# Output projection with five Strassen units in place of four: where the sums are made, which bank takes which product, and the order of the stage

## The chip, the core and the metric

The kernel runs on one core of a Trainium2 chip. The metric is the device time of one execution in microseconds (us). Three runs of the kernel before took 751.25, 751.36 and 752.31 us; the median is 751.36 us.

Five engines work side by side, each through its own instruction stream in order: TensorE (PE in the profile; PEld is its weight load), VectorE (DVE), ScalarE (ACT), GpSimd (POOL) and SyncE (SP, which here issues transfers). An instruction that must wait holds up everything behind it on its engine.

## The reference

```python
def _A_ref(x, wqkv, wo):                 # x: 1 x 2048 x 1024, 32 heads of 32
    q, k, v = split(x @ wqkv)
    phi = lambda t: where(t > 0, t + 1, exp(t)) + 1e-6
    pq, pk = phi(q), phi(k)
    kv = einsum("bhsd,bhse->bhde", pk, v)
    z = einsum("bhsd->bhd", pk)
    num = einsum("bhqd,bhde->bhqe", pq, kv)
    den = einsum("bhqd,bhd->bhq", pq, z)[..., None] + 1e-6
    return merge_heads(num / den) @ wo

def _B_ref(x, w_gate, w_up, w_down):     # 1024 -> 3584 -> 1024
    return (silu(x @ w_gate) * (x @ w_up)) @ w_down

xn = layernorm(x)
s = _A_ref(xn, wqkv, wo)
g = silu(_B_ref(xn, w_gate, w_up, w_down))
out = x + s * g
```

All tensors are bfloat16. The change lies in the last step of `_A_ref`, the product with `wo` (the output projection), which makes `s`.

## The kernel before, in words

The 2048 tokens are four blocks b = 0 to 3 of 512, each of four tiles t of 128 tokens. A 1024-wide row is eight chunks of 128 (G, DC); `wo` is cut into two column halves of 512 (CW), and HG = 4 is half of the chunks.

**Phase 1** makes the normalized, transposed input and the keys and values of all blocks (matmuls at L546) and sums them to KVZ (L568). **Phase 2** then goes through the blocks. `emit_Q` (L178 to 185) makes 128 columns of the queries of one block by eight matmuls into a PSUM tile, and `emit_phi` (L144 to 164) applies phi: for b > 0 three ACT steps (L148, L149, L150), then one DVE step (L151). `emit_ND` (L725 to 751) makes one tile's numerators and denominators with eight matmuls (L735) into the PSUM tile `nd`, then DVE divides: L739 and L743 make the reciprocals, L747 (three instructions) writes the quotient o. `nd` comes from a pool with one buffer of three PSUM banks (L387), so a later `nd` group waits until DVE has read an earlier one. `emit_OT` (L753 to 756) has SP issue a transposing transfer of o into `oT`, the left operand of the output projection.

**The output projection has two forms.** Directly, `emit_S` (L758 to 772): for one tile and one column half eight matmuls of 128x512 (L766), an ACT eviction with a scale (L769), and after the second half a store to `s_dram` from ACT's queue (L772). Blocks 0 and 1 go this way. Or as a unit of Strassen's method in Winograd's form, `s_unit` (L785 to 848): two token tiles together, seven products of four matmuls each (L808, called from `mmk`) where the direct form has 32 matmuls. The tiles of blocks 2 and 3 go this way, as pairs (0, 2) and (1, 3). A unit needs

- four differences of `wo`'s quarters, `To_sb`, made once by GpSimd (L774 to 780);
- four sums of `oT`'s quarters (`sums`, L801 to 804), made by DVE into a part of `wq_sb` that is no longer used (`so`) and, the fourth, in place into `oT`;
- four PSUM banks out of the five `fx`: X and Y change places from unit to unit, Z is always `fx[2]`, W is `fx[3]` or `fx[4]`.

Its products, by their names in the code: **x** into X, after which ACT copies X to Y (L814); **w** into W, after which ACT makes w1 (L821); **y** adds into Y, after which ACT copies Y to Z (L826) and makes s2 (L827); **x2** adds into X, evicted by ACT (L831); **z** adds into Z, evicted by DVE with w1 added (L835); **z2** adds further into Z, evicted by ACT (L840); **w2** adds into W, evicted by DVE with s2 added (L845). A tile's store is issued by SP (`out_s`, L852). The tiles w1 and s2 come from the pool `phiw`, whose tags "r_t" and "e_t" have two buffers each.

**The order is written out by hand.** PE, DVE, ACT and POOL run their instructions in program order (the manual schedule at L384), and SP too in this phase (L693). So the sequence of calls in L893 to L939 is the order of every engine. `run` takes a list of query groups and direct halves and puts the `nd` groups of the block before between them. After the last query group, L899 to L915 write out the tail of the direct form and the first unit, and L916 to L939 run the other three units from strings of steps: a bare name is a step of the unit n, "-" ahead of a name a step of the unit before it, `sums` the sums of the unit after, `nd` the next `nd` group with its transpose, `new` opens a unit, `Ssum` and `p` the DVE sums over the FFN's input (L688 to 692), `silu` loads ACT's table for the FFN.

Beside this, `prep_step` prepares the FFN's weights: DVE scales a tile (L311), GpSimd makes four differences of it (L323 to 326), and a store and further loads are issued. **Phase 3** is the FFN, the larger part of the kernel; its first products come from `emit_a` (L975), by matmuls at L958, with evictions at L985 and L986.

Of the kernel before, what the change touches and what calls it, by code (L numbers as in the profile page):

```python
# [9 lines left out]
ACT = mybir.ActivationFunctionType  # L10
ALU = mybir.AluOpType
FP32 = mybir.dt.float32
BF16 = mybir.dt.bfloat16
I32 = mybir.dt.int32
F32R = mybir.dt.float32r
F16 = mybir.dt.float16
# [5 lines left out]
def kernel(  # L22
# [11 lines left out]
    nc = tc.nc  # L34
    P = 128
    x2 = A_x.flatten_outer_dims()
    out2 = out.flatten_outer_dims()
    S, D = x2.shape
# [4 lines left out]
    DC = D // P  # L43
# [4 lines left out]
    TPB = TB // P  # L48
    CW = min(512, D)
# [48 lines left out]
    marks = {}  # L98
# [25 lines left out]
    wq_sb = w12.tile([P, DC, D], BF16, name="wq_sb")  # L124
# [8 lines left out]
    s_sc = persist.tile([P, 1], FP32, name="s_sc")  # L133
# [35 lines left out]
    phiw = p12.enter_context(tc.tile_pool(name="phiw", bufs=2, reuse_waits="tile"))  # L169
# [221 lines left out]
    with ExitStack() as p1:  # L391
        wpool = p1.enter_context(tc.tile_pool(name="p1w", bufs=1, reuse_waits="tile"))
        work = p1.enter_context(tc.tile_pool(name="p1work", bufs=2, reuse_waits="tile"))
# [222 lines left out]
        HG = G // 2  # L616
# [97 lines left out]
    with ExitStack() as p2:  # L714
# [43 lines left out]
        def emit_S(b, t, cc, bank=None):  # L758
            oT = oT_tiles[b]
            ttok = slice(t * P, (t + 1) * P)  # L760
            if (b, t) not in s_tiles:
                s_tiles[(b, t)] = work.tile([P, D], BF16, name="s_sb", tag="s_sb")
            s_sb = s_tiles[(b, t)]
            s_ps = bank or ps2.tile([P, CW], FP32, name="s_ps", tag="B2")
            for c in range(G):
                mm = nc.tensor.matmul(s_ps[:], lhsT=oT[:, c, ttok], rhs=wo_sb[:, c, cc * CW:(cc + 1) * CW],  # L766
                                      start=(c == 0), stop=(c == G - 1))
                marks.setdefault(("S", b, t), mm)
            nc.scalar.activation(out=s_sb[:, cc * CW:(cc + 1) * CW], in_=s_ps[:], func=ACT.Copy, scale=s_sc[:])  # L769
            if cc == NCC - 1:  # L770
                r0 = b * TB + t * P
                nc.scalar.dma_start(out=s_dram[r0:r0 + P, :], in_=s_tiles.pop((b, t))[:])  # L772
# [9 lines left out]
        fx = []  # L782
        unit_n = [0]

        def s_unit(b, u):  # L785
            n = unit_n[0]
            unit_n[0] += 1
            oT = oT_tiles[b]
            t1, t2 = u, u + 2
            k1, k2_ = slice(t1 * P, (t1 + 1) * P), slice(t2 * P, (t2 + 1) * P)  # L790
            a11, a12 = oT[:, 0:HG, k1], oT[:, HG:G, k1]
            a21, a22 = oT[:, 0:HG, k2_], oT[:, HG:G, k2_]
            b11, b21, b22 = wo_sb[:, 0:HG, 0:CW], wo_sb[:, HG:G, 0:CW], wo_sb[:, HG:G, CW:D]
            X, Y, Z, W = fx[n % 2], fx[1 - n % 2], fx[2], fx[3 + n % 2]
            so = wq_sb[:, TPB:DC, :].rearrange("p a b -> p (a b)")[:, (n % 2) * 2048:(n % 2) * 2048 + 3 * HG * P]
            so = so.bitcast(F16).rearrange("p (q k t) -> p q k t", q=3, k=HG)
            S4 = a21.bitcast(F16)
            sb = {}

            def sums():  # L800
                nc.vector.tensor_tensor(out=so[:, 0], in0=a21, in1=a22, op=ALU.add)  # L801
                nc.vector.tensor_tensor(out=so[:, 1], in0=so[:, 0], in1=a11, op=ALU.subtract)
                nc.vector.tensor_tensor(out=so[:, 2], in0=a11, in1=a21, op=ALU.subtract)
                nc.vector.tensor_tensor(out=S4, in0=a12, in1=so[:, 1], op=ALU.subtract)

            def mmk(out, a_, b_, first):
                for k in range(HG):
                    mm = nc.tensor.matmul(out[:], lhsT=a_[:, k, :], rhs=b_[:, k, :], start=first and k == 0,  # L808
                                          stop=k == HG - 1, skip_group_check=True)
                return mm  # L810

            def x():
                marks[("S", b, u)] = mmk(X, a11, b11, True)
                nc.scalar.copy(out=Y[:], in_=X[:])  # L814

            def w():
                for t in (t1, t2):
                    s_tiles[(b, t)] = work.tile([P, D], BF16, name="s_sb", tag="s_sb")
                mmk(W, so[:, 0], To[0], True)
                sb["w"] = phiw.tile([P, CW], FP32, name="w1", tag="r_t")  # L820
                nc.scalar.activation(out=sb["w"][:], in_=W[:], func=ACT.Copy, scale=s_sc[:])  # L821

            def y():
                mmk(Y, so[:, 1], To[1], False)
                s2 = sb["s2"] = phiw.tile([P, CW], FP32, name="s2", tag="e_t")
                nc.scalar.copy(out=Z[:], in_=Y[:])  # L826
                nc.scalar.activation(out=s2[:], in_=Y[:], func=ACT.Copy, scale=s_sc[:])  # L827

            def x2():
                mmk(X, a12, b21, False)  # L830
                nc.scalar.activation(out=s_tiles[(b, t1)][:, 0:CW], in_=X[:], func=ACT.Copy, scale=s_sc[:])  # L831

            def z():
                mmk(Z, so[:, 2], To[2], False)
                nc.vector.scalar_tensor_tensor(out=s_tiles[(b, t2)][:, CW:D], in0=Z[:], scalar=s_sc[:],  # L835
                                               in1=sb["w"][:], op0=ALU.mult, op1=ALU.add)

            def z2():
                mmk(Z, a22, To[3], False)
                nc.scalar.activation(out=s_tiles[(b, t2)][:, 0:CW], in_=Z[:], func=ACT.Copy, scale=s_sc[:])  # L840
                out_s(b, t2)

            def w2():
                mmk(W, S4, b22, False)
                nc.vector.scalar_tensor_tensor(out=s_tiles[(b, t1)][:, CW:D], in0=W[:], scalar=s_sc[:],  # L845
                                               in1=sb["s2"][:], op0=ALU.mult, op1=ALU.add)
                out_s(b, t1)
            return dict(sums=sums, x=x, w=w, y=y, x2=x2, z=z, z2=z2, w2=w2)

        def out_s(b, t):  # L850
            r0 = b * TB + t * P
# [22 lines left out]
        def mix(a, b_):  # L874
            r = []
            for k in range(max(len(a), len(b_))):
                r += a[k:k + 1] + b_[k:k + 1]
            return r

        def sh(b, hf):  # L880
            return [s_item(b, t, cc) for t in (2 * hf, 2 * hf + 1) for cc in range(NCC)]

        def run(body, at, b, order=(0, 1, 2, 3)):
            for k, f in enumerate(body):
                f()
                if k in at:
                    nd_item(b, order[at.index(k)])()
                phi_flush()

        def qs(b):  # L890
            return [q_item(b, g) for g in range(G)]

        run(qs(1), (1, 3, 5, 7), 0)  # L893
        q = qs(2)
        run(q[:2] + mix(q[2:], sh(0, 0) + sh(0, 1)), (1, 4, 7, 10), 1)
        q = qs(3)
        run(q[:2] + mix(q[2:], sh(1, 0)), (1, 4, 7, 10), 2, (0, 2, 1, 3))
        nds = [nd_item(3, t) for t in (0, 2, 1, 3)]
        emit_S(1, 2, 0)  # L899
        emit_S(1, 2, 1)  # L900
        fx.extend([ps2.tile([P, CW], FP32, name="fx%d" % k, tag="B2") for k in range(5)])
        units = [s_unit(2, 0), s_unit(2, 1)]
        u = units[0]
        nds[0]()
        u["x"]()
        u["sums"]()
        emit_S(1, 3, 0, fx[4])
        nds[1]()
        emit_S(1, 3, 1, fx[2])
        u["w"]()  # L910
        units[1]["sums"]()
        u["y"]()
        u["x2"]()
        nds[2]()
        u["z"]()  # L915
        parts = []  # L916
        for n in range(1, 4):
            u, v = units[n - 1], units[n]
            for st in ('x w nd new -z2 sums y -w2 x2 z', 'x w new Ssum -z2 sums p y -w2 x2 z p', 'x w -z2 y p -w2 z x2 p z2 silu w2')[n - 1].split():
                if st == "nd":  # L920
                    nds[3]()
                elif st == "new":
                    units.append(s_unit(3, n - 1))
                elif st == "sums":
                    units[n + 1]["sums"]()
                elif st == "p":
                    parts.pop(0)()
                elif st == "silu":
                    nc.scalar.preload_act_table(ACT.Silu)
                elif st == "Ssum":  # L930
                    blk_es.close()
                    blk12_es.close()
                    sp = ctx.enter_context(tc.tile_pool(name="p3S", bufs=1, side="right", reuse_waits="tile"))
                    emit_Ssum(passes[0], parts)
                    stat_ps[0] = lambda: psa_tile("st_ps3")[0][:, 0, 511:512]
                    prep_flush()
                elif st[0] == "-":
                    u[st[1:]]()
                else:  # L939
                    v[st]()  # L940
# [990 lines left out]
```

## Time and profile before

| | us |
|---|---|
| median of three runs | 751.36 |
| time of the profiled execution | 751.34 |
| its span in the trace | 749.6 |
| PE busy | 741.9 |
| PEld busy | 370.8 |
| DVE busy | 590.6 |
| POOL busy | 403.2 |
| ACT busy | 385.6 |
| first matmul of the stage's last query group starts / first FFN matmul starts | 208.88 / 244.28 |

The granted TensorE clock was 1.00 over the whole span. Times inside the trace count from the start of the span, in us; the profiled execution's own time is 1.7 us longer than the span. The rows used below have, in this order, start, duration, engine, line, operation, output<-inputs with partitions x elements and type, and the number of instructions taken together; a matmul's duration overlaps that of the next one, so the distance of starts tells PE's pace. In brackets stands idle time of the engine ahead of the row, and what ended it. POOL, DVE and ACT lines can be held against PE's by their start times, since all share one clock of the trace.

### The profile page before, as it was taken

The page shows a single profiled execution, that of the slowest core. Times are in us where ns is not written, and L with a number is a line of the kernel's source. Part 1 is how long each engine was busy: PE and PEld are TensorE (multiplying, and loading weights), DVE is VectorE, ACT ScalarE, POOL GpSimd, SP SyncE. Part 2 cuts the span into 40 slices and gives each one's busy share as a digit, 9 for nine tenths or more (in the row PEclk, how much of TensorE's full clock was granted, in tenths as well). Part 3 has the DMA queues.
Part 4 walks back from the last instruction along what each step waited for, and adds up shares of the span by engine and source line. Part 5 has one row for each costly group of instructions (what it writes and reads, how often), then busy time and mean ns, then how long its engine had stood idle before and what let it go on. Part 6 is the DMA issues. An engine that isn't in the chain of part 4 may idle for free.

```text
span 749.6 us, 11280 instructions
## 1 busy us (share of the span) xinstructions
PE 741.9 (99%) x3962; PEld 370.8 (49%) x3962; DVE 590.6 (79%) x1046; ACT 385.6 (51%) x556; POOL 403.2 (54%) x435
## 2 busy tenths in 40 slices
PE   8999999999999999999999999999999999999997
PEld 3544444454454444444444444644444444467665
DVE  6577788887697688788889886587877767688897
ACT  5677866889965666667557511232222232322023
POOL 0111799998640255858586027310766676770076
PEclk9999999999999999999999999999999999999999
DMA  9957799869678668787889417998698889668854
GB/s 316 337 139 149 219 329 307 310 151 263 208 202 273 229 223 289 274 322 279 320 270 417 169 48 295 269 373 282 225 306 305 307 290 347 244 221 315 279 172 92
DMA packets 132425, 194.21 MB, mean 259 GB/s; under 512 B 36384, under 2 KB 106144, under 8 KB 122640
## 3 DMA queue, kind: packets, MB, share of 16 engines
q1 hardware_dynamic: 123600, 158.69, 65.3%
q0 software_dynamic: 7328, 32.31, 11.6%
q10 hardware_dynamic: 1440, 2.49, 1.0%
q8 instruction: 31, 0.51, 0.3%
q14 instruction: 26, 0.21, 0.1%
HBM read 122.68 MB, written 63.96 MB: 249 GB/s over the span
## 4 chain that ended last, share of the span: by engine, by line
PE 94%; DVE 3%; DMA 1%; ACT 1%; issue 1%; POOL 1%; DVEq 0%; ACTq 0%; POOLq 0%; SPq 0%
PE zw L958 25%; PE kv_ps L546 15%; PE xb L958 13%; PE q_ps L183 6%; PE dzw L1252 6%; PE yb L958 6%; PE dm L1533 5%; PE dm L1497 3%; PE fx L808 3%; PE s_ps L766 3%; PE dx L1252 2%; PE dy L1252 2%; PE dm L1252 1%; PE kvz L568 1%; PE nd L735 1%
## 5 line engine op out<-in xcount | busy, mean ns | idle before, releaser
L958 PEld LDWEIGHTS <-w_sb 128*128 128x128 f16 (+1 forms) x1568 | 152.0, 98 | 183.1 <-issue 0.5
L958 PE MATMUL xb<-xnT,w_sb 128*128 128x512 bf16 x448 | 115.0, 379 | 0.0
L546 PE MATMUL kv_ps<-wkv_sb,xnT 128*128 128x512 bf16 x512 | 113.8, 379 | 0.6 <-ACT xnT L535 0.4
L958 PE MATMUL zw<-xnT,w_sb 128*128 128x512 bf16 x448 | 105.9, 379 | 0.0
L958 PE MATMUL zw<-S,w_sb 128*128 128x512 f16 x448 | 105.8, 379 | 0.0
L323 POOL TENSOR_TENSOR w_sb<-w_sb 128x512 f16<-128x512 bf16 x42 | 50.7, 1206 | 99.9 <-DVE w_sb L311 51.2
L288 ACT ACTIVATE w_sb<-w_sb 128x2048 bf16<-128x2048 bf16 x42 | 79.9, 1902 | 3.5 <-DMA w_sb<-in_B_w_up_dram 2.4
L546 PEld LDWEIGHTS <-xnT 128*128 128x128 bf16 x512 | 48.3, 97 | 56.0 <-ACT xnT L535 0.8
L1139 POOL TENSOR_TENSOR w_sb<-w_sb 128x512 f16<-128x512 f16 (+3 forms) x48 | 50.0, 1063 | 28.5 <-DMA w_sb<-wd 27.5
L1034 ACT ACTIVATE sg<-cg 128x1024 bf16<-128x1024 f32 x28 | 29.6, 1057 | 57.6 <-DVE cg L1027 57.6
L183 PE MATMUL q_ps<-xnT,wq_sb 128*128 128x512 bf16 x256 | 58.4, 379 | 0.4 <-DVE pqT L151 0.4
L958 PE MATMUL yb<-S,w_sb 128*128 128x512 f16 x224 | 57.5, 379 | 0.0
L1027 DVE SCALAR_TENSOR_TENSOR cg<-zw,rc_all,s 128x1024 f32<-128x1024 f32 x28 | 35.9, 1283 | 25.3 <-PE zw L958 12.8
L986 DVE SCALAR_TENSOR_TENSOR s<-yb,rc_all,s 128x512 f32<-128x512 f32 x42 | 31.4, 749 | 27.9 <-ACT s L985 27.9
L324 POOL TENSOR_TENSOR w_sb<-w_sb 128x512 f16<-128x512 bf16 x42 | 50.7, 1207 | 3.3
L1230 POOL DMA_DIRECT2D out_dram<-io x16 | 8.7, 544 | 80.7 <-DVE io L1229 80.5
L326 POOL TENSOR_TENSOR w_sb<-w_sb 128x512 f16<-128x512 bf16 x42 | 50.3, 1197 | 0.0
L325 POOL TENSOR_TENSOR w_sb<-w_sb 128x512 f16<-128x512 bf16 x42 | 49.8, 1185 | 0.0
L985 ACT ACTIVATE s<-xb,rcl 128x512 f32<-128x512 f32 x14 | 9.6, 687 | 65.0 <-PE xb L958 65.0
L985 ACT ACTIVATE s<-xb,rc_all 128x512 f32<-128x512 f32 x42 | 28.4, 675 | 21.9 <-issue 12.7
L311 DVE TENSOR_SCALAR w_sb<-w_sb,cs_all 128x2048 bf16<-128x2048 bf16 x35 | 36.2, 1035 | 3.5 <-DVE cs_all L301 0.8
L183 PEld LDWEIGHTS <-wq_sb 128*128 128x128 bf16 x256 | 24.4, 97 | 28.1 <-issue 0.6
(232 smaller groups left out, 1364.4 us busy)
## 6 DMA issues: line engine op xcount, KB each, us to landing
w_sb<-pk_g SPq DMA_DIRECT2D x27, 1024.0 KB, 6.4
pk_g<-w_sb SPq DMA_DIRECT2D x14, 1024.0 KB, 5.0
w_sb<-pk_u SPq DMA_DIRECT2D x14, 1024.0 KB, 8.5
pk_u<-w_sb POOLq DMA_DIRECT2D x13, 1024.0 KB, 5.5
w_sb<-l SPq DMA_DIRECT2D x12, 896.0 KB, 5.6
l<-w_sb POOLq DMA_DIRECT2D x9, 896.0 KB, 7.7
w_sb<-in_B_w_gate_dram SPq DMA_DIRECT2D x14, 512.0 KB, 6.6
w_sb<-in_B_w_down_dram SPq DMA_DIRECT2D x28, 256.0 KB, 4.7
```

The source lines that it names most:

```text
L183: nc.tensor.matmul(q_ps[:], lhsT=wq_sb[:, dc, g * P:(g + 1) * P], rhs=xn_ap(dc, btok), start=(dc == 0), stop=(dc == DC - 1))
L288: nc.scalar.activation(out=junk, in_=raw_view(key, t), func=ACT.Square, accum_out=asum[:])
L323: nc.gpsimd.tensor_tensor(out=T1, in0=b12, in1=b11, op=ALU.subtract)
L324: nc.gpsimd.tensor_tensor(out=T2, in0=b22, in1=T1, op=ALU.subtract)
L325: nc.gpsimd.tensor_tensor(out=T3, in0=b22, in1=b12, op=ALU.subtract)
L326: nc.gpsimd.tensor_tensor(out=T4, in0=b21, in1=T2, op=ALU.subtract)
L546: mm = nc.tensor.matmul(kv_ps[:], lhsT=xn_ap(dc, tok), rhs=wkv_sb[:, dc, c * CW:(c + 1) * CW], start=(dc == 0), stop=(dc == DC - 1))
L958: mm = nc.tensor.matmul(out, lhsT=lhs(k), rhs=rhs(k), start=(first and k == 0), stop=(k == HK - 1), skip_group_check=True)
L985: nc.scalar.activation(out=s1[:], in_=x_[:], func=ACT.Copy, scale=rc)
L1139: nc.gpsimd.tensor_tensor(out=b(o_), in0=b(a_), in1=b(b_), op=ALU.subtract)
L1252: nc.tensor.matmul(out, lhsT=lhs, rhs=rhs, start=first, stop=lastk, skip_group_check=True)
L1533: nc.tensor.matmul(out, lhsT=lhs, rhs=w[:, j], start=i == 1 and j == 0, stop=j == NQ - 1, skip_group_check=True)
```

## The change

- **A fifth unit.** Tiles 2 and 3 of block 1 become a unit, the new first one, in place of four calls of `emit_S` (two tiles, two halves). Units now are 0: block 1, tiles (2, 3); 1 and 2: block 2, tiles (0, 2) and (1, 3); 3 and 4: block 3, tiles (0, 2) and (1, 3).
- **Sums by GpSimd.** `s_unit` takes an engine for its sums. Units 0, 2 and 3 have GpSimd make them, units 1 and 4 DVE. Unit 0 makes its sums before the queries of block 3 (`early`), into two tiles of the tag "r_t", since `wq_sb` is still in use then; its w1 (same tag) is therefore read out of W only after y. Unit 2's sums are emitted ahead of the first step string. The sums can be emitted in two pairs, `suma` and `sumb`.
- **No copy from bank to bank after y.** z and z2 add into Y itself, after s2 has been read from it; bank Z and L826 are gone. X and Y rotate through `fx[0]`, `fx[1]`, `fx[3]`, and W is `fx[2]` or `fx[4]`. The copy from X to Y after x stays.
- **A new order** of the whole stage, in five strings. x2 is next behind x in units 1 and 2; unit 0 starts x, w, y, x2; the `nd` groups of block 3 stand behind unit 0's x2, between x2 and w of unit 1, at its end, and behind w of unit 2.

Line numbers move: 801 to 804 become 805, 806, 809, 810; 808 becomes 818; 814, 821, 827, 831, 835, 840, 845 become 824, 835, 840, 846, 850, 855, 860; 852 becomes 867; 958 becomes 964.

```diff
--- before.py
+++ after.py
@@ -782,26 +782,36 @@
         fx = []
         unit_n = [0]
 
-        def s_unit(b, u):
+        def s_unit(b, t1, t2, early=False, eng=nc.vector):
             n = unit_n[0]
             unit_n[0] += 1
             oT = oT_tiles[b]
-            t1, t2 = u, u + 2
             k1, k2_ = slice(t1 * P, (t1 + 1) * P), slice(t2 * P, (t2 + 1) * P)
             a11, a12 = oT[:, 0:HG, k1], oT[:, HG:G, k1]
             a21, a22 = oT[:, 0:HG, k2_], oT[:, HG:G, k2_]
             b11, b21, b22 = wo_sb[:, 0:HG, 0:CW], wo_sb[:, HG:G, 0:CW], wo_sb[:, HG:G, CW:D]
-            X, Y, Z, W = fx[n % 2], fx[1 - n % 2], fx[2], fx[3 + n % 2]
-            so = wq_sb[:, TPB:DC, :].rearrange("p a b -> p (a b)")[:, (n % 2) * 2048:(n % 2) * 2048 + 3 * HG * P]
-            so = so.bitcast(F16).rearrange("p (q k t) -> p q k t", q=3, k=HG)
+            if early:
+                se = [phiw.tile([P, 2, HG, P], F16, name="se%d" % k, tag="r_t") for k in range(2)]
+                so1, so2, so3 = se[0][:, 0], se[0][:, 1], se[1][:, 0]
+            else:
+                so = wq_sb[:, TPB:DC, :].rearrange("p a b -> p (a b)")[:, (n % 2) * 2048:(n % 2) * 2048 + 3 * HG * P]
+                so = so.bitcast(F16).rearrange("p (q k t) -> p q k t", q=3, k=HG)
+                so1, so2, so3 = so[:, 0], so[:, 1], so[:, 2]
+            X, Y, W = lambda: fx[(0, 3, 1)[n % 3]], lambda: fx[(1, 0, 3)[n % 3]], lambda: fx[2 + n % 2 * 2]
             S4 = a21.bitcast(F16)
             sb = {}
 
+            def sum_a():
+                eng.tensor_tensor(out=so1, in0=a21, in1=a22, op=ALU.add)
+                eng.tensor_tensor(out=so2, in0=so1, in1=a11, op=ALU.subtract)
+
+            def sum_b():
+                eng.tensor_tensor(out=so3, in0=a11, in1=a21, op=ALU.subtract)
+                eng.tensor_tensor(out=S4, in0=a12, in1=so2, op=ALU.subtract)
+
             def sums():
-                nc.vector.tensor_tensor(out=so[:, 0], in0=a21, in1=a22, op=ALU.add)
-                nc.vector.tensor_tensor(out=so[:, 1], in0=so[:, 0], in1=a11, op=ALU.subtract)
-                nc.vector.tensor_tensor(out=so[:, 2], in0=a11, in1=a21, op=ALU.subtract)
-                nc.vector.tensor_tensor(out=S4, in0=a12, in1=so[:, 1], op=ALU.subtract)
+                sum_a()
+                sum_b()
 
             def mmk(out, a_, b_, first):
                 for k in range(HG):
@@ -810,42 +820,47 @@
                 return mm
 
             def x():
-                marks[("S", b, u)] = mmk(X, a11, b11, True)
-                nc.scalar.copy(out=Y[:], in_=X[:])
-
-            def w():
+                marks[("S", b, t1)] = mmk(X(), a11, b11, True)
+                nc.scalar.copy(out=Y()[:], in_=X()[:])
                 for t in (t1, t2):
                     s_tiles[(b, t)] = work.tile([P, D], BF16, name="s_sb", tag="s_sb")
-                mmk(W, so[:, 0], To[0], True)
+
+            def w():
+                mmk(W(), so1, To[0], True)
+                if not early:
+                    w_copy()
+
+            def w_copy():
                 sb["w"] = phiw.tile([P, CW], FP32, name="w1", tag="r_t")
-                nc.scalar.activation(out=sb["w"][:], in_=W[:], func=ACT.Copy, scale=s_sc[:])
+                nc.scalar.activation(out=sb["w"][:], in_=W()[:], func=ACT.Copy, scale=s_sc[:])
 
             def y():
-                mmk(Y, so[:, 1], To[1], False)
+                mmk(Y(), so2, To[1], False)
                 s2 = sb["s2"] = phiw.tile([P, CW], FP32, name="s2", tag="e_t")
-                nc.scalar.copy(out=Z[:], in_=Y[:])
-                nc.scalar.activation(out=s2[:], in_=Y[:], func=ACT.Copy, scale=s_sc[:])
+                nc.scalar.activation(out=s2[:], in_=Y()[:], func=ACT.Copy, scale=s_sc[:])
+                if early:
+                    w_copy()
 
             def x2():
-                mmk(X, a12, b21, False)
-                nc.scalar.activation(out=s_tiles[(b, t1)][:, 0:CW], in_=X[:], func=ACT.Copy, scale=s_sc[:])
+                mmk(X(), a12, b21, False)
+                nc.scalar.activation(out=s_tiles[(b, t1)][:, 0:CW], in_=X()[:], func=ACT.Copy, scale=s_sc[:])
 
             def z():
-                mmk(Z, so[:, 2], To[2], False)
-                nc.vector.scalar_tensor_tensor(out=s_tiles[(b, t2)][:, CW:D], in0=Z[:], scalar=s_sc[:],
+                mmk(Y(), so3, To[2], False)
+                nc.vector.scalar_tensor_tensor(out=s_tiles[(b, t2)][:, CW:D], in0=Y()[:], scalar=s_sc[:],
                                                in1=sb["w"][:], op0=ALU.mult, op1=ALU.add)
 
             def z2():
-                mmk(Z, a22, To[3], False)
-                nc.scalar.activation(out=s_tiles[(b, t2)][:, 0:CW], in_=Z[:], func=ACT.Copy, scale=s_sc[:])
+                mmk(Y(), a22, To[3], False)
+                nc.scalar.activation(out=s_tiles[(b, t2)][:, 0:CW], in_=Y()[:], func=ACT.Copy, scale=s_sc[:])
                 out_s(b, t2)
 
             def w2():
-                mmk(W, S4, b22, False)
-                nc.vector.scalar_tensor_tensor(out=s_tiles[(b, t1)][:, CW:D], in0=W[:], scalar=s_sc[:],
+                mmk(W(), S4, b22, False)
+                nc.vector.scalar_tensor_tensor(out=s_tiles[(b, t1)][:, CW:D], in0=W()[:], scalar=s_sc[:],
                                                in1=sb["s2"][:], op0=ALU.mult, op1=ALU.add)
                 out_s(b, t1)
-            return dict(sums=sums, x=x, w=w, y=y, x2=x2, z=z, z2=z2, w2=w2)
+            return dict(sums=sums, sum_a=sum_a, sum_b=sum_b, x=x, w=w, y=y, x2=x2, z=z, z2=z2, w2=w2)
 
         def out_s(b, t):
             r0 = b * TB + t * P
@@ -893,34 +908,25 @@
         run(qs(1), (1, 3, 5, 7), 0)
         q = qs(2)
         run(q[:2] + mix(q[2:], sh(0, 0) + sh(0, 1)), (1, 4, 7, 10), 1)
+        units = [s_unit(1, 2, 3, early=True, eng=nc.gpsimd)]
+        units[0]["sums"]()
         q = qs(3)
         run(q[:2] + mix(q[2:], sh(1, 0)), (1, 4, 7, 10), 2, (0, 2, 1, 3))
         nds = [nd_item(3, t) for t in (0, 2, 1, 3)]
-        emit_S(1, 2, 0)
-        emit_S(1, 2, 1)
         fx.extend([ps2.tile([P, CW], FP32, name="fx%d" % k, tag="B2") for k in range(5)])
-        units = [s_unit(2, 0), s_unit(2, 1)]
-        u = units[0]
-        nds[0]()
-        u["x"]()
-        u["sums"]()
-        emit_S(1, 3, 0, fx[4])
-        nds[1]()
-        emit_S(1, 3, 1, fx[2])
-        u["w"]()
-        units[1]["sums"]()
-        u["y"]()
-        u["x2"]()
-        nds[2]()
-        u["z"]()
+        units += [s_unit(2, 0, 2), s_unit(2, 1, 3, eng=nc.gpsimd)]
+        units[2]["sums"]()
         parts = []
-        for n in range(1, 4):
+        for n in range(5):
             u, v = units[n - 1], units[n]
-            for st in ('x w nd new -z2 sums y -w2 x2 z', 'x w new Ssum -z2 sums p y -w2 x2 z p', 'x w -z2 y p -w2 z x2 p z2 silu w2')[n - 1].split():
+            for st in ('x w y x2 nd', 'suma -z x x2 sumb nd w y -z2 -w2 z nd', 'x x2 w nd new -z2 sums y -w2 z',
+                       'x w new Ssum -z2 sums p y -w2 x2 z p', 'x w -z2 y p -w2 z x2 p z2 silu w2')[n].split():
                 if st == "nd":
-                    nds[3]()
+                    nds.pop(0)()
                 elif st == "new":
-                    units.append(s_unit(3, n - 1))
+                    units.append(s_unit(3, n - 2, n, eng=nc.gpsimd if n == 2 else nc.vector))
+                elif st in ("suma", "sumb"):
+                    v["sum_" + st[3]]()
                 elif st == "sums":
                     units[n + 1]["sums"]()
                 elif st == "p":
```

## The prediction, made before the changed kernel ran

> **What bounds the kernel now.** I read the page first, busy shares and chain of waits, then TensorE's (PE's) timeline through the stage that changes.
>
> ```profile
> PE 741.9 (99%) x3962; PEld 370.8 (49%) x3962; DVE 590.6 (79%) x1046; ACT 385.6 (51%) x556; POOL 403.2 (54%) x435
> ...
> PE 94%; DVE 3%; DMA 1%; ACT 1%; issue 1%; POOL 1%; DVEq 0%; ACTq 0%; POOLq 0%; SPq 0%
> ```
>
> PE is busy for 741.9 of 749.6 us and carries 94% of the chain. A matmul less is time won, and any wait that PE gets is time lost unless something absorbs it later; with PE dense from 245 us on, nothing does. So I set the old and the new order of PE between 208.88 us (last query product) and 244.28 us (first product of the FFN) against each other. Columns: start, duration, engine, line, output<-inputs, count.
>
> ```profile
> 208.88 1.89 PE L183 MATMUL q_ps<-xnT,wq_sb 128*128 128x512 bf16 x8
> 210.61 3.62 PE L766 MATMUL s_ps<-wo_sb,oT 128*128 128x512 bf16 x16
> 214.06 0.63 PE L735 MATMUL nd<-KVZ,pqT 128*128 128x132 bf16 x8
> ...
> 224.09 1.02 PE L808 MATMUL fx<-To_sb,wq_sb 128*128 128x512 f16 x4
> 225.20 0.64 PE L735 MATMUL nd<-KVZ,pqT 128*128 128x132 bf16 x8
> 225.94 1.02 PE L808 MATMUL fx<-To_sb,oT 128*128 128x512 f16 x4
> ...
> 241.49 1.02 PE L808 MATMUL fx<-wo_sb,oT 128*128 128x512 bf16 x4
> 242.55 1.02 PE L808 MATMUL fx<-To_sb,oT 128*128 128x512 f16 x4
> ```
>
> Take starts, since the durations overlap. Sixteen matmuls take 3.45 us (210.61 to 214.06): 0.216 each, 0.863 for a product of a unit (four), 0.47 for an nd group (214.06 to 214.53). After 224.09 the next start is due at 224.95 and comes at 225.20; after 225.20, due 225.67, comes 225.94; after 241.49, due 242.35, comes 242.55. So PE waits here 0.25 + 0.27 + 0.20 = 0.72 us in all, and that is what a better order can win besides matmuls.
>
> **What is removed.** Four direct half-tile outputs (32 matmuls) become one unit (28): 4 x 0.216 = **0.86 us**. The copy from Y to Z (L826, 0.57 us of ACT) goes, but z now waits until ACT has read Y into s2. The first two waits, 0.52 us, go too, since other work stands there; the third stays (z, x2, z2 follow each other in the last unit as before).
>
> **What is added: a product right behind the copy of its bank.** The new order starts unit 0 with x, w, y, x2, and units 1 and 2 with x and x2 next to each other. x2 adds into the bank that ACT must first copy to Y, so PE waits for that copy, and PE takes nothing out of order: the nd group behind x2 waits as well. ACT's rows:
>
> ```profile
> 210.81 0.60 ACT L148 ACTIVATE e_t<-q_ps 128x512 f32<-128x512 f32 x1
> 211.43 0.63 ACT L149 ACTIVATE e_t<-e_t 128x512 f32<-128x512 f32 x1
> 211.97 0.58 ACT L150 ACTIVATE q_ps<-q_ps 128x512 f32<-128x512 f32 x1
> ...
> 237.42 0.57 ACT L814 COPY fx<-fx 128x512 f32<-128x512 f32 x1 [1.09 <-PE fx L808]
> ```
>
> The x of that copy started at 236.30, so ACT gets a product 1.12 us after its start; the copy takes 0.57, and PE follows an evacuation by 0.05 (L835 starts 241.75, takes 0.75; PE at 242.55). x2 can start 1.12 + 0.57 + 0.05 = 1.74 us after x, where PE is there after 0.863: a wait of **0.86 us** with a margin of 0.06, in unit 1 and again in unit 2 (before, w or more stood between).
>
> Unit 0 has w between x and y, but ACT is not free: its queue holds the three steps of the last query tile (rows above), ending 212.55, where the old kernel had eight direct matmuls running. The copy runs from about 212.48 to 213.05, y starts at 213.10, and PE was ready at 210.61 + 2 x 0.863 = 212.34: **0.76 us**.
>
> z behind y and one other product starts 1.12 + 0.69 (s2 instead of the shorter copy) + 0.05 = 1.86 after y, where PE is there after 1.73: 0.13 in the last unit and 0.12 in unit 2. In units 1 and 3 more stands between.
>
> **What is moved: sums to GpSimd.** Unit 0's four sums find GpSimd idle: its timeline shows nothing from 189.64 to 195.79, four operations of 1.15 take 4.6 us, and the last transpose they need was issued at 185.51 and landed 4.5 us later, at 190.0. Done by 194.7: no cost. If they ran late, the weight sums due at 195.79 would slip, which feed stores of weights and no matmul of this stage. Unit 2's four sums come behind GpSimd's last weight sums, which end at 217.90, and run 217.9 to about 223. Unit 2 needs them only at 228: hidden from PE. But they meet VectorE, which makes unit 1's four sums just then. GpSimd, then VectorE:
>
> ```profile
> 216.75 1.15 POOL L326 TENSOR_TENSOR w_sb<-w_sb 128x512 f16<-128x512 bf16 x1
> ...
> 445.20 3.12 POOL L1127 TENSOR_TENSOR w_sb<-w_sb 128x256 f16<-128x256 bf16 x4
> ```
>
> ```profile
> 216.80 1.38 DVE L801 TENSOR_TENSOR wq_sb<-oT 128x512 f16<-128x512 bf16 x1
> ...
> 446.21 0.77 DVE L1088 TENSOR_TENSOR hT<-hT,hs 128x512 f16<-128x512 bf16 x1
> 446.90 0.89 DVE L1085 TENSOR_TENSOR hs<-hT 128x512 f16<-128x512 bf16 x1
> 447.82 0.77 DVE L1086 TENSOR_TENSOR hs<-hs,hT 128x512 f16<-128x512 f16 x1
> 448.52 0.41 DVE L1087 TENSOR_TENSOR hs<-hT 128x512 f16<-128x512 bf16 x1
> ```
>
> A sum takes 0.42 alone. L801 met a GpSimd sum and ended at 218.18, 0.28 after that one (217.90). From 445.2 to 448.3 four GpSimd sums stand against VectorE sums, and one VectorE sum ends per GpSimd sum: they take turns. L747, which reads PSUM, took its usual 1.35 beside GpSimd.
>
> I carry this through. The waits so far put nd(3,0) at 214.83 (before 214.06); VectorE follows 0.67 later with 0.41 + 0.39 + 1.35 us for that tile, so unit 1's first sum arrives at 218.04, behind a GpSimd sum begun at 217.9. Taking turns, with GpSimd sums of about 1.33 when they give way, the sums end near 219.35, 220.76, 222.08 and 223.4. PE's w of unit 1 waits for the first: **0.27** (ready 219.22, 0.14 behind the sum). y waits for the second: **0.55**. nd(3,1) reuses the PSUM tile of nd(3,2), whose VectorE work is queued behind the fourth sum and ends 2.15 after it, at 225.55: PE is ready at 224.35, waits until 225.6: **1.25**. Bounds for these 2.07 us: nothing if the engines do not meet, 4 x 0.96 (1.38 less 0.42) if every sum pays as L801 did without overlap. I take 2.07, by the row with four turns.
>
> The Trainium skill, SBUF — State Buffer, "Who interferes with whom", says that a VectorE operation with two SBUF inputs and a GpSimd one that reads SBUF exclude each other, whoever comes second waiting for the whole of the first. Read strictly, the second then still has its full 0.42 us to run, where L801 shows 0.28; by that the four turns end 4 x 0.14 = 0.56 us later and the sum below is 4.0 instead of 3.4. I go by the row.
>
> Unit 3's sums (GpSimd) wait for transposes that can start only after unit 0's last read of its buffer, at about 223.8 instead of 219.5. The second is issued at 225.6 and lands 3.0 to 5.7 us later (the transposes' view for 219 to 230), at most 231.3; the first sum is needed at 234.4, one per 1.2 us: covered. Two stores move from ACT's queue to SP's, behind two of the transposes; they are 256 KB each and no one near waits.
>
> **Sum.** -0.86 - 0.52 + 0.76 + 0.86 + 0.86 + 0.12 + 0.13 + 2.07 = **+3.42 us**. FFN starts at 247.7 instead of 244.28, and all behind it shifts. The profiled execution took 751.34 (span 749.6 and 1.7 around it), 0.02 under the median 751.36: **754.8 us**, +0.45%.
>
> **Rivals.** About 0.2%, 1.5 us, is what a measurement of this kernel can tell from no change.
>
> (1) *No meeting of the two engines*, so not slower by that measure. Place: unit 1's sums. If VectorE's sums get through as if alone, the 2.07 goes and +1.35 stays: 752.7, +0.18%. It decides if GpSimd's sums start after 219.8, or if VectorE slips through the gap between two of them. For it: two of the old L801 rows ran 0.41 with GpSimd idle. Against: the rows at 445 us. Chance 0.18.
>
> (2) *A late transpose.* The last, nd(3,3)'s, is issued near 232.4, and VectorE's sums of unit 4 wait for it with the evacuations of units 2 and 3 queued behind. Landing 3.0 to 4.7 us later costs nothing; at 5.7 it holds z2 of unit 3 by about 1.0, at the 6.3 that the same view shows as longest, by 1.5: 755.8 to 756.3. For it: the transpose issued at 219.50 took 5.7. Against: the last two of the old stage took 3.1. Chance 0.11.
>
> (3) *The copies cost nothing and neither do the sums*: all waits gone, -0.86 - 0.72 = -1.58, 749.8. It would need ACT to copy within 0.86 of x's start, where every L814 row has 1.06 or more before it begins. Chance 0.04.
>
> (4) Only one or two of the turns are paid: 753.2 to 754.2, chance 0.12; the forecast itself 0.55.
>
> The range goes from 752.2 (0.5 under 1, since the terms of 1 were each read to about 0.1) to 756.3, the end of 2; it leaves out 3 and the outer part of 1. Chances: faster 0.04; same 0.18 (half of 1 may come out over the bound, a part of 4 under it); slower 0.78.
>
> **What would show it.** In the new profile: PE starts x2 of units 1 and 2 1.7 us after x; ACT's first copy begins right at 212.5; unit 1's VectorE sums take 0.9 to 1.4 us each with GpSimd's at 1.3; nd(3,1) waits for VectorE; the first FFN matmul starts at 247.7. Wrong: two copies without a PE gap, or sums of 0.42 beside busy GpSimd.

## The result and the profile after

The changed kernel took **754.19 us** (median of six runs, 753.95 to 754.85) against 751.36 us before: a ratio of **1.0037** with a 95% interval of 1.0024 to 1.005, so +2.83 us. The forecast was 754.8, with 752.2 to 756.3 as its range. In the profiled execution (753.95 us, span 752.2) the first FFN product starts at 246.80, where the forecast had 247.7 and the kernel before 244.28.

TensorE's timeline of the new stage; every piece that came more than 0.5 us late is kept (the bracket gives idle time and its releaser, "..." marks rows left out):

```profile
210.55 1.03 PE L818 MATMUL fx<-wo_sb,oT 128*128 128x512 bf16 x4
211.41 1.03 PE L818 MATMUL fx<-To_sb,se 128*128 128x512 f16 x4
213.01 1.02 PE L818 MATMUL fx<-To_sb,se 128*128 128x512 f16 x4 [0.58 <-ACT fx L824]
...
217.81 1.02 PE L818 MATMUL fx<-wo_sb,oT 128*128 128x512 bf16 x4 [0.71 <-ACT fx L824]
...
224.18 0.64 PE L735 MATMUL nd<-KVZ,pqT 128*128 128x132 bf16 x8 [0.57 <-DVE wq_sb L747]
224.66 1.02 PE L818 MATMUL fx<-wo_sb,oT 128*128 128x512 bf16 x4
226.40 1.02 PE L818 MATMUL fx<-wo_sb,oT 128*128 128x512 bf16 x4 [0.71 <-ACT fx L824]
...
231.86 1.02 PE L818 MATMUL fx<-To_sb,wq_sb 128*128 128x512 f16 x4 [0.52 <-ACT s L840]
...
246.80 1.03 PE L964 MATMUL yb<-S,w_sb 128*128 128x512 f16 x4
```

The bracket undercounts, because a matmul's duration overlaps the next one; a wait is read as start less due start, with 0.863 for a product and 0.47 for an nd group, as in the forecast. For example y of unit 0: 211.41 + 0.86 = 212.27 due, 213.01 come, 0.74. The whole stage:

| wait of TensorE | forecast | measured |
|---|---|---|
| y of unit 0 (copy behind the last phi) | 0.76 | 0.74 |
| x2 of unit 1, x2 of unit 2 (copy of the bank) | 0.86, 0.86 | 0.88, 0.88 |
| w, y of unit 1 (sums on VectorE) | 0.27, 0.55 | 0, 0 |
| nd(3,1) (the same sums) | 1.25 | 0.73 |
| z of unit 2 | 0.12 | 0.69 |
| z of unit 4, z2 of unit 4 | 0.13, 0.20 | 0.08, 0.20 |
| sum | 5.00 | 4.20 |

Before, the waits came to 0.72. So the stage got 4.20 - 0.72 - 0.86 (four matmuls less) = 2.62 us longer; the trace has (246.80 - 208.82) - (244.28 - 208.88) = 2.58. The two profiled executions differ by 753.95 - 751.34 = 2.61, so that is the whole of their difference; the medians differ by 2.83.

The sums. VectorE's four for unit 1, with the eviction between them; then GpSimd's last weight difference (L326) and the first three of its four for unit 2:

```profile
217.47 0.70 DVE L805 TENSOR_TENSOR wq_sb<-oT 128x512 f16<-128x512 bf16 x1
218.21 1.26 DVE L806 TENSOR_TENSOR wq_sb<-wq_sb,oT 128x512 f16<-128x512 f16 x1
219.40 0.74 DVE L850 SCALAR_TENSOR_TENSOR s_sb<-fx,s_sc,w 128x512 bf16<-128x512 f32 x1
220.06 0.71 DVE L809 TENSOR_TENSOR wq_sb<-oT 128x512 f16<-128x512 bf16 x1
220.80 1.26 DVE L810 TENSOR_TENSOR oT<-oT,wq_sb 128x512 f16<-128x512 bf16 x1
```

```profile
216.75 1.15 POOL L326 TENSOR_TENSOR w_sb<-w_sb 128x512 f16<-128x512 bf16 x1
217.85 1.34 POOL L805 TENSOR_TENSOR wq_sb<-oT 128x512 f16<-128x512 bf16 x1
219.27 1.22 POOL L806 TENSOR_TENSOR wq_sb<-wq_sb,oT 128x512 f16<-128x512 f16 x1
220.45 1.33 POOL L809 TENSOR_TENSOR wq_sb<-oT 128x512 f16<-128x512 bf16 x1
```

Read the ends. GpSimd's rows end at 217.90, 219.19, 220.49, 221.78; VectorE's four sums at 218.17, 219.47, 220.77, 222.06: each 0.27 to 0.28 after one of GpSimd's. They do take turns. VectorE's first sum, begun 0.38 before GpSimd's first, had only the end of the weight difference to wait for (0.70 us, where a sum alone takes 0.42); three, not four, stood behind GpSimd's sums.

The late z of unit 2 has a cause that the forecast did not have. The chain of waits from 224.18 on (start, length, what):

```profile
224.18 0.64 PE nd L735 x8
224.82 0.73 PE fx L818 x4
225.56 3.72 DMA s_dram<-s_sb
229.28 0.02 issue
229.30 0.04 ACTq L846
229.34 0.05 issue
229.38 0.07 ACT s_sb L846
...
231.23 0.59 ACT s L840
231.81 0.04 issue
231.86 1.24 PE fx L818 x5
```

A store of unit 0's output tile, issued at 225.56 and landed at 229.28, stands on the chain. ScalarE's eviction L846 of unit 2 writes into the same buffer of the pool `s_sb` (four buffers; the changed kernel's units take two each) and so could not start before 229.38. Behind it in ScalarE's queue stand w1, z2's eviction and s2 (L840), and z waits for s2.

### The profile page after: what moved, and what is told of

Read it like the earlier page. It is cut to its first block, busy times and chain, and to the rows that moved or that the text cites. A ratio compares the mean times of both kernels' runs of the same rounds, so it can differ in the third digit from the quotient of the medians.

```text
span 752.2 us, 11279 instructions
## 1 busy us (share of the span) xinstructions
PE 741.8 (99%) x3958; PEld 370.9 (49%) x3958; DVE 591.3 (79%) x1040; ACT 384.1 (51%) x553; POOL 418.1 (56%) x447
## 4 chain that ended last, share of the span: by engine, by line
PE 94%; DMA 2%; DVE 2%; ACT 1%; issue 0%; SPq 0%; DVEq 0%; ACTq 0%
PE zw L964 26%; PE kv_ps L546 14%; PE xb L964 13%; PE yb L964 6%; PE q_ps L183 6%; PE dzw L1258 6%; PE dm L1539 6%; PE dm L1503 4%; PE fx L818 3%; PE s_ps L766 2%; PE dy L1258 2%; PE dx L1258 2%; PE dm L1258 1%; DMA wkv_sb<-in_A_wqkv_dram 1%; PE kvz L568 1%; PE nd L735 1%
## 5 line engine op out<-in xcount | busy, mean ns | idle before, releaser
L288 ACT ACTIVATE w_sb<-w_sb 128x2048 bf16<-128x2048 bf16 x42 | 79.9, 1902 | 7.8 <-DMA w_sb<-in_B_w_up_dram 7.8
L326 POOL TENSOR_TENSOR w_sb<-w_sb 128x512 f16<-128x512 bf16 x42 | 50.4, 1200 | 0.0
```

The costliest lines, as they stand in the source:

```text
L288: nc.scalar.activation(out=junk, in_=raw_view(key, t), func=ACT.Square, accum_out=asum[:])
L326: nc.gpsimd.tensor_tensor(out=T4, in0=b21, in1=T2, op=ALU.subtract)
```

## The experiments

Times of whole kernels differ here by little more than a run's scatter, so each run is read twice: by its ratio to the kernel before, timed on the same chip, and by the trace, as the **stage length** from unit 0's x to the first FFN product. The changed kernel has 246.80 - 210.55 = **36.25 us**; what follows behind the stage took 505.1 to 506.6 us in all the profiles. A ratio's interval is 0.6 to 1 us to each side; for the runs compared with the changed kernel the two readings agree within 0.4 us in all but one, which is named.

### w between x and x2 in unit 2

```diff
-'x x2 w nd new -z2 sums y -w2 z'
+'x w x2 nd new -z2 sums y -w2 z'
```

> Edit: in unit 2 the product w stands between x and x2 (order x w x2 nd instead of x x2 w nd). Theory A: the wait of 0.88 us between x and x2 goes, since w fills it, but only part of it is won: ScalarE still waits for the store's slot until 229.38, then evicts x2, z2 and makes s2, which ends at about 231.3, so z starts near 231.35 instead of 231.86. That is about 0.5 us: 753.7. Rival B: the two waits are independent, and the full 0.88 is won: 753.3.

753.47 us, ratio 1.0026 (1.0016 to 1.0035). Stage 35.53, 0.72 us less. The wait of 0.88 is gone; the nd group behind takes a part of it back, and z waits a little less than before. TensorE, then ScalarE:

```profile
226.29 1.02 PE L818 MATMUL fx<-wo_sb,oT 128*128 128x512 bf16 x4
227.45 0.64 PE L735 MATMUL nd<-KVZ,pqT 128*128 128x132 bf16 x8
...
231.10 1.02 PE L818 MATMUL fx<-To_sb,wq_sb 128*128 128x512 f16 x4 [0.42 <-ACT s L840]
```

```profile
229.20 0.69 ACT L846 ACTIVATE s_sb<-fx,s_sc 128x512 bf16<-128x512 f32 x1 [2.04 <-DMA s_dram<-s_sb]
```

The first row is x2, without a wait now. nd(3,3) behind it is 0.30 late (227.45 less 226.29 + 0.86; it needs the tile that VectorE still reads for nd(3,1)), and z still waits 0.59 (0.69 in the changed kernel). The copy is confirmed as the cause of the 0.88. The gain lies between the two theories: the store holds ScalarE as theory A says, but in this execution only until 229.20, not 229.38, and w1 (0.57) is out of the way by then, so z comes 0.76 sooner.

### GpSimd first at the sums

```diff
-'suma -z x x2 sumb nd w y -z2 -w2 z nd'
+'-z suma x x2 sumb nd w y -z2 -w2 z nd'
```

> Edit: unit 1's first two VectorE sums are put behind the eviction of unit 0's z (order -z suma instead of suma -z), so that VectorE's first sum comes at about 218.1, after GpSimd has begun its own at 217.85, where in the changed kernel it came at 217.47, ahead of it. No work is added. Theory A (the two engines take turns, and the order of arrival decides how many turns VectorE pays): VectorE's sums end 0.28 us behind GpSimd's, at about 219.5, 220.8, 222.1 and 223.4; w of unit 1 waits about 0.3, y about 0.4, and nd(3,1) about 1.3 us instead of 0.73 (less what the eviction, already done, gives back): 0.6 to 1.4 us more in all, 754.8 to 755.6. Rival B (the sums are only slowed in proportion to the overlap): the swap costs nothing that is seen, 754.0 to 754.4.

755.15 us, ratio 1.0047 (1.0034 to 1.006). Stage 37.37: **1.12 us more** for two VectorE operations that stand behind a third instead of ahead of it. VectorE, then GpSimd:

```profile
217.99 1.09 DVE L805 TENSOR_TENSOR wq_sb<-oT 128x512 f16<-128x512 bf16 x1
219.11 1.26 DVE L806 TENSOR_TENSOR wq_sb<-wq_sb,oT 128x512 f16<-128x512 f16 x1
220.29 1.37 DVE L809 TENSOR_TENSOR wq_sb<-oT 128x512 f16<-128x512 bf16 x1
221.70 1.26 DVE L810 TENSOR_TENSOR oT<-oT,wq_sb 128x512 f16<-128x512 bf16 x1
```

```profile
217.64 1.16 POOL L805 TENSOR_TENSOR wq_sb<-oT 128x512 f16<-128x512 bf16 x1
218.88 1.21 POOL L806 TENSOR_TENSOR wq_sb<-wq_sb,oT 128x512 f16<-128x512 f16 x1
```

Now all four VectorE sums stand behind one of GpSimd's sums (the first ends at 219.08, 0.28 after GpSimd's 218.80), and TensorE waits 0.15 at w, 0.43 at y and 1.19 at nd(3,1), where the forecast for this very case had 0.27, 0.55 and 1.25. Slowing in proportion to the overlap is ruled out: the work is the same, only the order of arrival differs, and all four ends again stand 0.28 behind GpSimd's.

### Unit 2's sums back on VectorE

```diff
-units += [s_unit(2, 0, 2), s_unit(2, 1, 3, eng=nc.gpsimd)]
-units[2]["sums"]()
+units += [s_unit(2, 0, 2), s_unit(2, 1, 3)]
-'suma -z x x2 sumb nd w y -z2 -w2 z nd'
+'suma -z x x2 sumb nd sums w y -z2 -w2 z nd'
```

> Edit: unit 2's four sums go back from GpSimd to VectorE, behind nd(3,2) in VectorE's queue; GpSimd is then idle while VectorE makes unit 1's sums. Theory A (the sums on GpSimd cost more than they take off VectorE, since the two take turns): unit 1's sums run at 0.42 us each and end near 219.8 instead of 222.06, nd(3,1) starts on time, 0.73 us are won although VectorE has four more sums to make: 753.4. Rival B (VectorE is what is short in this stretch): the four added sums, 1.7 us, delay its evictions, nd(3,3) or z waits in their place, and the time is 754.2 or more.

753.15 us, ratio 1.0023 (1.0013 to 1.0032). The eight sums run at 0.42 us each but for the first (0.64, against the last weight difference), and nd(3,1) starts on time. But the profiled execution, one of the longer ones of this kernel (753.95), has a stage of 36.14, only 0.11 less (the ratio says about 1 us): z of unit 2 waits 1.31 there. ScalarE:

```profile
229.25 0.69 ACT L846 ACTIVATE s_sb<-fx,s_sc 128x512 bf16<-128x512 f32 x1 [3.66 <-DMA s_dram<-s_sb]
```

The store that frees the buffer was issued at 226.79, behind two transposes that SP took 2.43 and 1.42 us to issue (1.23 and 1.31 in the changed kernel), and landed at 229.14, no later than the changed kernel's (229.28). So ScalarE starts about when it did there, while TensorE comes to z 0.76 us sooner: what was won at nd(3,1) is lost again at z. The two causes are coupled, and the next runs part them.

### Five output buffers

```diff
-work = p2.enter_context(tc.tile_pool(name="p2work", bufs=4, ...
+work = p2.enter_context(tc.tile_pool(name="p2work", bufs=5, ...
```

> Edit: the pool of the output tiles s_sb gets five buffers instead of four; nothing else changes. (Six buffers do not fit in the space that is left.) Theory A (the store's slot is the term that the forecast left out): in the changed kernel ScalarE waits up to 229.38 to write unit 2's first half-tile, because the buffer still belongs to unit 0's tile, whose store lands at 229.28; with that s2 is late and TensorE's z of unit 2 waits 0.69 us. With five buffers that half-tile has a free one, the wait becomes the forecast 0.12, and 0.57 us are won: about 753.6. Rival B (ScalarE is full there anyway): z still waits 0.6 to 0.7 us, 754.2.

753.76 us, ratio 1.0028 (1.0017 to 1.004). Stage 35.58, 0.67 less. ScalarE, and with it z:

```profile
227.38 0.69 ACT L846 ACTIVATE s_sb<-fx,s_sc 128x512 bf16<-128x512 f32 x1 [1.11 <-PE fx L818]
```

It now waits for its product and not for a store, starts at 227.38 instead of 229.38, and z is 0.08 late instead of 0.69. The slot of the store was the missing term.

### Both: five buffers, and unit 2's sums on VectorE

The edit is the two diffs above together.

> Edit: unit 2's sums on VectorE behind nd(3,2), as in the run of that name, and five output buffers, as in the other. Theory A: the run with the sums on VectorE did remove the 0.73 us at nd(3,1), and lost it again because the store that holds the buffer was issued later; with a fifth buffer both are won, nd(3,1) starts on time and z of unit 2 waits about 0.1 us: from unit 0's x to the first FFN product 34.9 to 35.0 us, where the changed kernel has 36.25 and the kernel before (with its two direct halves there) 33.67; time about 1.3 us under the changed kernel. Rival B: VectorE with four more sums is late for something else (nd(3,3), z), and less than 0.9 us is won.

752.90 us, ratio 1.0015 (1.0006 to 1.0024). Stage 245.87 - 210.96 = 34.91, as theory A had it. Left are the waits 0.74, 0.88, 0.88, 0.08, 0.07 and 0.21. With five buffers GpSimd's help with unit 2 thus cost 35.58 - 34.91 = 0.67 us (0.73 in the changed kernel) and saved TensorE nothing. The theory's words on the store are half right: it was issued later, but it did not land later, as the run with the sums on VectorE alone shows.

### Unit 1's sums on GpSimd too, ahead of the weight differences

```diff
-units += [s_unit(2, 0, 2), s_unit(2, 1, 3, eng=nc.gpsimd)]
+units += [s_unit(2, 0, 2, eng=nc.gpsimd), s_unit(2, 1, 3, eng=nc.gpsimd)]
+units[1]["sums"]()
 units[2]["sums"]()
+late_T.pop()()          # the last four weight differences, held back until here
-'suma -z x x2 sumb nd w y -z2 -w2 z nd'
+'-z x x2 nd w y -z2 -w2 z nd'
```

> Edit: unit 1's sums go to GpSimd too, ahead of unit 2's, and the four weight differences that stood before them in GpSimd's queue go behind both (they feed no product of this stage). VectorE makes no sums until unit 4. Theory A: no VectorE sum meets a GpSimd one, nd(3,1) starts on time, 0.73 us are won, 753.4; the first sum of unit 1 is done near 213.8, long before w. Rival B (GpSimd's eight sums in a row, 1.15 us each, end near 222 and are late for w or y): TensorE waits on GpSimd instead, 754.2 or more.

753.07 us, ratio 1.0022 (1.0013 to 1.0031). Stage 35.50, 0.75 less, which is the wait at nd(3,1). GpSimd makes the eight sums from 212.20 to 222.06 at 1.15 us each, the first in 1.61, and none is late. So the engines may share the work, as long as their sums do not meet.

### A direct half behind the last query group

```diff
-run(q[:2] + mix(q[2:], sh(1, 0)), (1, 4, 7, 10), 2, (0, 2, 1, 3))
+s4 = sh(1, 0)
+run(q[:2] + mix(q[2:], s4[:3]) + s4[3:], (1, 4, 7, 9), 2, (0, 2, 1, 3))
```

> Edit: the last direct half of block 1 (eight products and one eviction) goes from between the query groups to behind the last of them, so that TensorE has 1.7 us of it while ScalarE makes the last phi. Theory A: ScalarE's copy of X no longer stands behind phi, y of unit 0 starts without a wait, and 0.74 us are won: 753.4; the nd group ahead of the last query group comes 1.7 us sooner and must not wait for VectorE. Rival B: the copy is late for another reason or the nd groups wait in its place: no gain, 754.2.

754.00 us, ratio 1.003 (1.0019 to 1.0041). Stage 35.88, 0.37 less, half of what was expected. The copy did come free of phi, but two things took its place: w of unit 0 is 0.30 late (it waits for the eviction of the moved half, which ScalarE ends at 211.69; w starts at 211.75), and y still 0.10 (the copy starts at 212.10, behind that eviction and the issue of its store). An nd group is 0.13 late besides.

### All causes together

> Edit: five units as in the changed kernel, with all the causes taken away together: five output buffers; sums of units 0 to 3 by GpSimd, with the last four weight differences behind them; w between x and x2 in units 1 and 2; one direct half behind the last query group. Theory A (the terms add): left of the changed kernel's 4.20 us of waits are about 0.40 at unit 0 (as in the run with the half last), 0.12 in unit 2 and 0.28 in unit 4, so 3.4 us less than the changed kernel: 750.8 us, level with the kernel before or up to 0.1% below it. Rival B (each wait removed shows another one behind it, as the nd group did in the run with w between): 751.5 to 752.5.

The edit joins five buffers, GpSimd's sums for units 0 to 3 with the last weight differences behind them, the half moved, and `'-z x w x2 nd y ...'`, `'x w x2 nd ...'`. 751.24 us, ratio 0.9996 (0.9987 to 1.0004), level with the kernel before. Stage 32.91, **3.34 less** than the changed kernel (3.4 expected): the terms add. Four fifths of the changed kernel's waits are gone, the 0.88 of unit 1 in this run for the first time.

### A better order

```diff
+def first_x():                       # ahead of the last query group
+    fx.extend(...)
+    units[0]["x"]()
+body[-1] = lambda: emit_Q(3, G - 1, bank=fx[3])
-'x w y x2 nd'
+'w y x2 nd'
-'x w -z2 y p -w2 z x2 p z2 silu w2'
+'x w -z2 y p -w2 z x2 p w2 z2 silu'
```

(on top of the run with all causes, with the half back in its old place)

> Edit: as the run with all causes taken away, but the direct half stays among the query groups and unit 0's x is put ahead of the last query group instead (that group is made in a fifth fx bank), so that ScalarE's copy of X stands ahead of the last phi and not behind it; in the last unit w2 stands between x2 and z2. Theory A: unit 0 then waits nowhere (0.39 us in the run with all causes taken away) and the last z2 does not wait for VectorE (0.20 us); left are about 0.06, 0.07 and 0.08 us. From the start of the last query group, with unit 0's x counted in, to the first FFN product: 34.0 us, where the kernel before has 35.4. Time 1.4 us below the kernel before, about 0.18%. Rival B: the phi of the last group, now 0.86 us later, makes VectorE's last pqT late and nd(3,0) waits for it: 0.5 to 1 us less is won, and the time is within 0.1% of the kernel before.

**750.35 us**, ratio 0.9983 (0.9974 to 0.9992): 0.17% faster than the kernel before. From unit 0's x at 208.66, which follows the last nd group of block 2, to the first FFN product at 242.74 it takes 34.08 us, where the kernel before has 208.88 to 244.28, 35.40. ScalarE's copy stands ahead of the last phi now:

```profile
209.91 0.58 ACT L150 ACTIVATE q_ps<-q_ps 128x512 f32<-128x512 f32 x1
210.42 0.53 ACT L825 COPY fx<-fx 128x512 f32<-128x512 f32 x1
211.45 0.60 ACT L148 ACTIVATE e_t<-fx 128x512 f32<-128x512 f32 x1 [0.49 <-PE fx L183]
```

and TensorE goes through w and y at 211.25 without a wait. In this execution 0.72 us of it were given back at 392.50, where a product (L292) waits for ScalarE (L288), which waits for a weight load that took 7.95 us from issue to landing (6.86 in the kernel before). The same place cost 0.53 us in the run with all causes together and 0.62 in the run with five buffers and VectorE's sums, where the FFN started later than in the kernel before, so it isn't a price of being early; what makes the load slow wasn't tried.

### The kernel before without its copy from Y to Z

```diff
-X, Y, Z, W = fx[n % 2], fx[1 - n % 2], fx[2], fx[3 + n % 2]
+X, Y, W = fx[(0, 2, 1)[n % 3]], fx[(1, 0, 2)[n % 3]], fx[3 + n % 2]
-nc.scalar.copy(out=Z[:], in_=Y[:])     # z and z2 use Y
```

> Edit: the kernel before, with only the copy from bank Y to bank Z left out: z and z2 add into Y after s2 was read, and three banks take turns as X and Y. Theory A (the copy was hidden; without it z waits for s2 where only one product stands between y and z): 0.1 us more in the last unit, nothing elsewhere, time as before within 0.1%. Rival B (ScalarE's 0.57 us per unit was on the path): up to 0.5 us less.

751.60 us, ratio 0.9996 (0.9987 to 1.0005). From the last query group to the first FFN product 35.48 instead of 35.40: the one new wait is 0.07 at z of the last unit. The copy was hidden, and leaving it out is neutral.

## Why the prediction was right, and which terms were off

**Matmuls and old waits, -0.86 - 0.52: right.** The two waits at nd and z are gone, the third, 0.20, stands at 245.07. **Copies, +0.76 + 0.86 + 0.86: right**, 0.74, 0.88 and 0.88; these 2.5 us are nearly the whole net loss, and the last order won them back. **z behind y, +0.13 in unit 4: right** in kind, 0.08.

**Sums on two engines, +2.07: mis-sized, 0.73.** The mechanism holds to 0.01 us (each VectorE sum ends 0.27 to 0.28 after a GpSimd operation). The step that failed is "unit 1's first sum arrives at 218.04, behind a GpSimd sum begun at 217.9": it came at 217.47, ahead of GpSimd's 217.85. That was to be had from the forecast's own numbers, 214.83 + 0.67 + 0.41 + 0.39 + 1.35 = 217.65; the 218.04 has the 0.39 twice. So it went ahead of GpSimd's first sum and took 0.28 us longer than alone, for the end of the weight difference, instead of a whole turn. One turn less, about 1.3 us, is the difference, and the run that put GpSimd first paid it, with 1.77 us of waits where 2.07 were forecast. The outcome lies between the forecast and rival 4: three turns paid, not one or two, at a price (0.73) within the 0.5 to 1.5 of rival 4. By the sums alone the time would have been 752.7 + 0.73 = 753.4; half a microsecond of the rest is the next term.

**z of unit 2, +0.12: wrong, 0.69.** The step was "Two stores move from ACT's queue to SP's, behind two of the transposes; they are 256 KB each and no one near waits." ScalarE waits for their buffer. The forecast looked at who reads what is stored, not at who writes next into the tile. In the total it made up for 0.57 of the 1.34 us by which the sums were overrated; that much of the agreement is luck. What made the landing late shows in the traces, though no run changed it: in all ten profiles with five units this store landed 0.53 to 0.73 us behind the second of the two transposes ahead of it in SP's queue (229.28 behind 228.67 in the changed kernel), whether it was issued 2.26 or 3.89 us before.

The transposes of rival 2 came early: the last was issued at 230.97 and landed at 234.00, and no eviction was held. Unit 0's sums cost nothing, as forecast, and the missing copy no more than the 0.08.

The rule weighed in the forecast (the Trainium skill, SBUF — State Buffer, "Who interferes with whom": whoever comes second waits for the whole of the first) holds as far as the turns go. That the second then still needs its full time does not show: in seven turns of two kernels VectorE's sum ended 0.28 us after GpSimd's, where a sum alone takes 0.42. The measurement decides.

## What to carry to other kernels

On a path without slack, an accumulation that goes on in a bank which another engine must first copy costs product latency, copy and hand-over less the work that stands between: put one product of another bank there. Before giving sums to GpSimd, lay them on VectorE's timeline: where they meet VectorE sums each turn costs a whole GpSimd operation (about 1.3 us here), and a few tenths in the order of arrival decide how many turns are paid. And a moved store is not free when nobody waits for its data: ask who writes next into its buffer.

## What was not expected of the hardware

GpSimd gives way as well: beside VectorE's sums its own take 1.21 to 1.34 us instead of 1.15 (the forecast had allowed 1.33). SP's issue of one transposing transfer took 1.2 to 1.8 us at most places and 2 us or more at others, in every profile: 2.01 and 2.08 at 200.85 and 206.59 in the kernel before, 2.43 at 222.76 in the run with unit 2's sums on VectorE, 3.49 at 179.00 in the run with a half behind the last query group. Why was not tried.
